# Windowed tiles of v transferred over 128 partitions instead of 112

## The chip, the cores and the metric

The kernel runs on one core of one Trainium2 chip. The metric is the device time of one execution in microseconds (us). The kernel before was timed in three runs: 497.3, 494.58 and 493.47 us, median 494.58.

## The reference, cut to what matters

Three layers follow one another. First comes an attention over q, k and v (4 batches, 8 heads, 576 positions, 64 wide) that adds a local part and a part on averaged positions:

```python
mask = np.abs(pos[:, None] - pos[None, :]) < 4
scores = np.where(mask, scale * q @ k.T, -1e9)
out_local = softmax(scores) @ v
q_d, k_d, v_d = means of 4 neighbouring positions
out_up = np.repeat(softmax(scale * q_d @ k_d.T) @ v_d, 4, axis=2)
x = out_up + out_local
```

Its output, as 2304 rows of 512, goes through `g(x @ w_in) @ w_out`, where g is a ratio of polynomials in its argument and w_in and w_out are 512x2048 and 2048x512. The result feeds a soft mixture of 8 experts (phi, w1, w2), which gives the output. Because the local part sees only 3 neighbours on each side, 32 queries need 38 positions of k and v.

## The kernel before, in words

**Attention.** The work goes in 16 pairs of heads. Each pair has three loads, all issued by SP. `load_qk` (line 538) brings q and k (`in_qk`, 128 partitions x 1158 f32). `load_v` (lines 540 to 542) brings two things: v for the averaged part (`in_vd`, 72 rows filled up to 80, x 1024 f32), which is added up over four positions on POOL (L570, L571) or DVE, and v for the local part (`in_vw`, `VROWS` = 112 rows x 1280 f32):

```python
begin(out=s.Vdl, in_=vd[bb, p])
begin(out=s.V[0:VROWS], in_=vw[bb, p])
```

`in_vw` is made on the host (lines 1531 to 1534 and 1538). v is cut into 18 overlapping tiles of 38 positions. Four tiles after four, two of them side by side, lie one above the other: the first two at partitions 0 to 37, the next two at partitions 64 to 101. The rows between and behind are zeros. TensorE reads only those two groups of 38 partitions (`av`, line 643). Line 1538 cuts the array to 112 rows.

For a pair, TensorE computes the local scores (`sc`, L576, L580) and the averaged ones (`scd`, L590). DVE takes the maxima (L595), ACT the exponentials (L598, L602), DVE and POOL the normalisation (L612, L613, L617). TensorE transposes (L623, L632) and multiplies with v (`avd` L650, `av` L643), and DVE adds both parts (L667).

**Weights.** w_in and w_out arrive as 64-bit floats, 1 MB for 256 columns or rows (`wst`, eight loads of each). DVE turns them into 32-bit floats in three steps (`nar`: L756, L761, L765). ACT and POOL split w_in further (L729, L734). w_out is stored to a tile in DRAM (`wo_dram`) and read back later.

**Order.** The order of all instructions on every engine is fixed by hand (`PLACE`), so an instruction that waits holds up all that stands behind it on its engine. SP issues nearly all transfers, in order, at line 427 (`begin`). Before some loads it also waits until an older load has landed: going back over the loads before, it adds up planned durations until they reach 4.5 us, and waits for the load found there (`LIMIT`, `GATED`, lines 353 to 359, and line 429). So a load that lands late makes a later one start late. The first four pairs use four sets of buffers and are loaded together with the first weights, in the first 55 us. From the fifth pair on each pair's loads wait until the buffers of the one before are free.

**Later.** After the first 60 us TensorE multiplies with w_in (`hps`, L889), while ACT, DVE and POOL compute g (`gate`, L965 to L994). The remaining pairs of the attention are worked in between, until about 310 us. The experts' weights (`we`, 32 loads of 1 MB) and the last layer follow.

Of the kernel before, what the change touches and what calls it, by code (L numbers as in the profile page):

```python
# [15 lines left out]
B, H, S, D = 4, 8, 576, 64  # L16
# [5 lines left out]
PAD = 3  # L22
QT = 32
WIN = QT + 2 * PAD
VROWS = 112
NEG = -8.0e9
EPS = 1e-9
COLS = ((0, 256), (256, 128), (384, 128))
# [377 lines left out]
def attn_moe_moe_kernel(ctx, tc, qk, vw, vd, w_in, w_out, w1, w2, cf, cb, out):  # L406
# [18 lines left out]
    def begin(out, in_):  # L425

        x = nc.sync.dma_start(out=out, in_=in_)
        if plan.gate.get(plan.item) in begun and plan.item not in begun:
            tc.add_manual_dep(x.ins, begun[plan.gate[plan.item]].ins.name, GATE, reason="few loads at once")
        begun[plan.item] = x  # L430
# [109 lines left out]
    def load_v(s, bb, p):  # L540
        begin(out=s.Vdl, in_=vd[bb, p])
        begin(out=s.V[0:VROWS], in_=vw[bb, p])

# [1038 lines left out]
```

## Time and profile before

| | |
|---|---|
| median of three runs | 494.58 us (493.47 to 497.3) |
| the profiled execution, its own time | 496.0 us |
| its span, from the first instruction to the last | 494.2 us |
| granted TensorE clock, mean | 0.979 |
| TensorE matmul busy | 460.3 us, 93% |
| DVE / ACT / POOL busy | 401.0 / 321.2 / 246.8 us |
| bytes moved by DMA | 88.50 MB |

Times in the trace count from the start of the span. The profiled execution took 1.8 us more than its span, and 1.4 us more than the median of the three runs. A busy share is a mean over the whole span; the first 60 us look different from the rest.

### The profile page before, as it was taken

The numbers are of one execution on the slowest core, as the hardware profiler recorded it, in microseconds if no ns is written. First come the engines' busy times: TensorE is split into PE (matmuls) and PEld (weight loads), VectorE is DVE, ScalarE is ACT, GpSimd is POOL, SyncE is SP. The second block draws the span as 40 slices with busy tenths as digits, with TensorE's granted clock in tenths as the row PEclk, the third lists the DMA queues.
The fourth block names the chain that finished last, engine by engine and source line by source line (L and its number), as shares of the span: only waits on it lengthen the run. The fifth ranks groups of instructions, "written<-read, shape, count | busy, mean of one in ns | idle before, by whom it ended". The sixth has DMA issues, their size and how long they took to land.

```text
span 494.2 us, 12949 instructions
## 1 busy us (share of the span) xinstructions
PE 460.3 (93%) x5417; PEld 335.1 (68%) x5417; DVE 401.0 (81%) x568; ACT 321.2 (65%) x682; POOL 246.8 (50%) x231
## 2 busy tenths in 40 slices
PE   7677889999999999999999999999999999799994
PEld 5455656787777777866777676777776976343574
DVE  5697999999999899958888799899899988736133
ACT  3664388788776778867779776667866576710122
POOL 6587777875874557577174656624142605101000
PEclk9799899999999999999999999999999999999898
DMA  8999915476555101312402322380000499999956
GB/s 333 299 281 319 324 51 221 138 235 215 147 156 164 52 27 53 118 51 76 122 1 76 97 61 72 128 316 1 0 1 0 165 383 354 388 426 426 426 221 237
DMA packets 17610, 88.50 MB, mean 179 GB/s; under 512 B 2064, under 2 KB 2576, under 8 KB 10896
## 3 DMA queue, kind: packets, MB, share of 16 engines
q1 hardware_dynamic: 17552, 87.67, 50.6%
q8 instruction: 43, 0.70, 0.6%
q14 instruction: 15, 0.12, 0.1%
HBM read 78.75 MB, written 8.91 MB: 177 GB/s over the span
## 4 chain that ended last, share of the span: by engine, by line
PE 42%; DVE 21%; POOL 12%; ACT 11%; DMA 9%; issue 4%; SPq 0%; DVEq 0%; POOLq 0%; ACTq 0%
PE hps L889 15%; POOL gate L971 7%; DMA at<-in_qk 5%; PE op L1451 3%; DVE gate L990 3%; ACT hps L989 3%; PE gt L1018 3%; PE hps L907 2%; DMA wst<-in_w_in 2%; POOL gate L967 2%; ACT gate L988 2%; DMA wo_dram<-wo 2%; ACT gate L975 2%; PE hp L1330 2%; PE scd L590 2%
## 5 line engine op out<-in xcount | busy, mean ns | idle before, releaser
L889 PE MATMUL hps<-XH,W 128*128 128x512 f32 x512 | 169.4, 400 | 2.4 <-DVE wst L765 1.8
L889 PEld LDWEIGHTS hps<-XH,W 128*128 128x128 f32 x512 | 96.6, 189 | 28.8 <-issue 2.5
L971 POOL TENSOR_TENSOR gate<-gate 128x1024 f32<-128x1024 f32 (+1 forms) x34 | 81.1, 2386 | 47.1 <-ACT gate L965 21.9
L889 PE MATMUL hps<-XL,W 128*128 128x512 f32 x256 | 100.7, 393 | 0.2
L967 POOL TENSOR_SCALAR gate<-gate,cf_sb 128x1024 f32<-128x1024 f32 (+1 forms) x25 | 32.2, 1289 | 71.9 <-ACT gate L975 70.4
L988 ACT ACTIVATE gate<-gate,one 128x1024 f32<-128x1024 f32 (+1 forms) x37 | 42.0, 1136 | 33.1 <-POOL gate L971 32.1
L990 DVE SCALAR_TENSOR_TENSOR gate<-gate,hps 128x1024 f32<-128x1024 f32 (+1 forms) x37 | 44.0, 1188 | 14.0 <-ACT hps L989 13.5
L889 PEld LDWEIGHTS hps<-XL,W 128*128 128x128 f32 x256 | 48.4, 189 | 9.8 <-POOL XL L734 0.9
L989 ACT ACTIVATE hps<-gate 128x1024 f32<-128x1024 f32 (+1 forms) x37 | 37.2, 1006 | 8.9 <-DVE gate L987 4.1
L729 ACT COPY G<-gt 128x512 f32<-128x512 f32 x56 | 32.7, 590 | 9.7 <-PE gt L1018 9.4
L564 POOL TENSOR_TENSOR at<-at 128x144 f32<-128x144 f32 x56 | 35.5, 634 | 4.4
L975 ACT ACTIVATE gate<-hps 128x1024 f32<-128x1024 f32 (+1 forms) x29 | 29.0, 999 | 5.4 <-PE hps L889 4.2
L971 DVE TENSOR_TENSOR gate<-gate,hps 128x1024 f32<-128x1024 f32 x24 | 29.1, 1214 | 4.0 <-ACT gate L965 3.8
L1018 PE MATMUL gt<-cf_sb,gate 128*128 128x128 f32 x192 | 28.7, 278 | 2.5 <-ACT G L729 1.1
L1018 PEld LDWEIGHTS gt<-cf_sb,gate 128*128 128x128 f32 x192 | 21.7, 141 | 11.3 <-ACT G L729 3.8
L602 ACT ACTIVATE at<-sc,at 128x38 f32<-128x38 f32 x144 | 28.2, 315 | 0.6
L987 DVE SCALAR_TENSOR_TENSOR gate<-gate,cf_sb,hps 128x1024 f32<-128x1024 f32 x22 | 28.1, 1276 | 0.6
L994 DVE SCALAR_TENSOR_TENSOR gate<-gate 128x1024 f32<-128x1024 f32 x20 | 26.0, 1298 | 0.4
L617 POOL TENSOR_TENSOR at<-at 128x432 f32<-128x432 f32 (+1 forms) x24 | 20.3, 852 | 12.0 <-DVE at L613 8.7
L965 ACT ACTIVATE gate<-hps,cf_sb 128x1024 f32<-128x1024 f32 x19 | 23.0, 1208 | 4.0 <-PE gt L1018 2.6
L907 PE MATMUL hps<-xs,W 128*128 128x256 f32 x192 | 24.3, 285 | 1.3 <-DVE A L993 1.2
L993 DVE SCALAR_TENSOR_TENSOR gate<-gate,cf_sb,hps 128x1024 f32<-128x1024 f32 x20 | 25.5, 1273 | 0.0
(182 smaller groups left out, 983.5 us busy)
## 6 DMA issues: line engine op xcount, KB each, us to landing
we<-in_w SPq DMA_DIRECT2D x32, 1024.0 KB, 9.5
at<-in_qk SPq DMA_DIRECT2D x16, 579.0 KB, 5.2
at<-in_vw SPq DMA_DIRECT2D x16, 560.0 KB, 5.2
wst<-in_w_in SPq DMA_DIRECT2D x8, 1024.0 KB, 9.5
wst<-in_w_out SPq DMA_DIRECT2D x8, 1024.0 KB, 5.9
at<-in_vd SPq DMA_DIRECT2D x16, 320.0 KB, 5.7
out<-late SPq DMA_DIRECT2D x17, 256.0 KB, 2.4
wo_dram<-wo SPq DMA_DIRECT2D x8, 512.0 KB, 8.0
```

The costliest lines, as they stand in the source:

```text
L564: nc.gpsimd.tensor_tensor(out=dst, in0=dst, in1=x[:, :, j], op=ALU.add)
L602: nc.scalar.activation(out=dst[:, i, :], in_=st["s", j][:, i, :], func=ACTF.Exp, scale=scale, bias=mx[:, i:i + 1], accum_out=None if sums ...
L729: nc.scalar.copy(out=out, in_=x)
L889: nc.tensor.matmul(hps[m][:, c].rearrange("p u t -> p (u t)"), lhsT=W[p][:, w, kk, 128 * c:128 * c + 128], rhs=x[xx][:, kk, :], start=(kk ...
L907: nc.tensor.matmul(out[:, c, :], lhsT=W[p][:, w, kk, 128 * c:128 * c + 128], rhs=xs[i][:, xx, kk, :], start=(kk == 0 and j == 0), stop=(kk ...
L967: (nc.vector if who == "d" else nc.gpsimd).tensor_scalar(out=out, in0=x, scalar1=coef[:, w:w + 1], scalar2=coef[:, b:b + 1], op0=ALU.mult, ...
L971: turned_over((nc.vector if who == "d" else nc.gpsimd).tensor_tensor(out=out, in0=x, in1=y, op=op), who)
L975: do("ab", "B", "H", lambda B, H: act(out=B, in_=H, func=ACTF.Abs, scale=coef[:, 4:5] if s2 else 1.0))
L988: do("ln", "C", "B", lambda C, B: act(out=C, in_=B, func=ACTF.Ln, bias=one))
L989: do("ex", "H", "C", lambda H, C: act(out=H, in_=C, func=ACTF.Exp, scale=-1.0))
L990: do("e", "B", "H", lambda B, H: stt(out=B, in0=B, scalar=1.0 + 1e-6, in1=H, op0=ALU.add, op1=ALU.mult))
L1018: nc.tensor.transpose(gt[n][:, u, 128 * c:128 * c + 128], g_of(n, c)[:, 128 * u:128 * u + 128], idn)
```

## The change

`VROWS` goes from 112 to 128, and the host no longer cuts the array. The tile in SBUF has 128 partitions already. Each of the 16 `in_vw` loads moves 128 x 1280 x 4 = 655,360 bytes instead of 573,440. The 16 rows more are zeros that nothing reads.

```diff
-VROWS = 112
+VROWS = 128
...
-        "vw": flat(win, B, H // 2, 128, 1280)[:, :, 0:VROWS].copy(),
+        "vw": flat(win, B, H // 2, 128, 1280),
```

The instructions of TensorE, DVE, ACT and POOL stand in the same order with the same waits. On SP only the shape of 16 rows differs. Here is the place on SP of the first of them; `at` is the buffer, the names in brackets are semaphores that the row waits for.

```order
 L427 DMA at<-in_qk 128x1158 [waits DMAHW4_49]
 L427 DMA at<-in_vd 80x1024
-L427 DMA at<-in_vw 112x1280 [waits DMAHW1_49]
+L427 DMA at<-in_vw 128x1280 [waits DMAHW1_49]
 L427 DMA wst<-in_w_in 128x2048 [waits DMAHW6_49]
```

Nothing moved: the load waits for what it waited for, and the same loads stand ahead of and behind it.

## Rows read from the trace of the kernel before

**Rows 1.** The page: DMA busy tenths in 40 slices of 12.4 us; the chain by engine.
```profile
DMA  8999915476555101312402322380000499999956
...
PE 42%; DVE 21%; POOL 12%; ACT 11%; DMA 9%; issue 4%; SPq 0%; DVEq 0%; POOLq 0%; ACTq 0%
```
**Rows 2.** Chain that ended last, 0 to 60 us: start us, us, what.
```profile
9.07 9.02 DMA at<-in_qk
...
26.56 9.19 DMA wo_dram<-wo
...
35.77 7.41 DMA at<-in_qk
...
43.19 10.76 DMA wst<-in_w_in
```
**Rows 3.** Timeline of DVE, 10 to 60 us; in brackets idle before, and its releaser.
```profile
19.57 0.52 DVE L595 TENSOR_REDUCE at<-sc 128x9 f32<-128x342 f32 x1 [1.08 <-PE sc L580]
...
23.54 0.61 DVE L595 TENSOR_REDUCE at<-scd 128x3 f32<-128x432 f32 x1 [2.32 <-PE scd L590]
...
38.16 1.23 DVE L756 TENSOR_SCALAR nar<-wst 128x1024 int32<-128x1024 int32 x1 [0.64 <-DMA wst<-in_w_in]
...
47.29 0.69 DVE L756 TENSOR_SCALAR nar<-wst 128x512 int32<-128x512 int32 x1 [2.00 <-DMA wst<-in_w_in]
...
54.05 0.69 DVE L756 TENSOR_SCALAR nar<-wst 128x512 int32<-128x512 int32 x1 [0.70 <-DMA wst<-in_w_in]
```
**Rows 4.** Busy time by stretch; last columns PEclk, DMA share, GB/s.
```profile
9.00:14.00 5.00, 3.29 (x182) 2.45 (x169) 4.34 (x9) 4.31 (x22) 3.34 (x7) 1.00 0.99 409
14.00:19.00 5.00, 1.65 (x92) 1.37 (x95) 4.15 (x9) 3.75 (x21) 1.63 (x2) 0.73 1.04 277
...
21.00:27.00 6.00, 5.26 (x102) 3.92 (x100) 3.61 (x6) 5.55 (x22) 3.95 (x7) 0.82 1.03 249
28.00:32.00 4.00, 3.48 (x33) 1.97 (x32) 3.97 (x9) 1.36 (x3) 3.48 (x3) 1.00 0.99 246
...
39.00:44.00 5.00, 4.62 (x99) 3.38 (x96) 4.86 (x5) 3.71 (x7) 1.93 (x4) 1.00 0.99 406
44.00:51.00 7.00, 3.96 (x87) 3.17 (x86) 4.86 (x9) 1.46 (x4) 6.69 (x8) 0.71 1.03 252
...
56.00:60.00 4.00, 3.97 (x18) 2.96 (x17) 3.83 (x9) 1.64 (x2) 3.44 (x4) 1.00 1.05 229
```
**Rows 5.** Timeline of SP, 0 to 60 us: the issue of transfers.
```profile
9.93 0.42 SPq L427 DMA_DIRECT2D at<-in_vw  x1
...
18.53 0.90 SPq L427 DMA_DIRECT2D at<-in_vw  x1
...
25.54 0.43 SPq L427 DMA_DIRECT2D at<-in_vw  x1
...
32.45 2.10 SPq L427 DMA_DIRECT2D wst<-in_w_in  x2
...
36.20 0.53 SPq L427 DMA_DIRECT2D wst<-in_w_in  x1
...
38.53 0.47 SPq L427 DMA_DIRECT2D at<-in_vw  x1
...
54.40 0.42 SPq L427 DMA_DIRECT2D at<-in_vw  x1
```
**Rows 6.** Tensor in_vw, 180 to 320 us (7 loads): who waited (nobody listed), and landing.
```profile
who waited for it (us, times):
busy tenths in 40 slices 0000000000000000000000000000000000000000
DMA to landing us min/median/max: 3.9/4.2/5.1
```
**Rows 7.** Tensor in_qk, 160 to 300 us (6 loads): landing.
```profile
DMA to landing us min/median/max: 3.7/3.9/5.1
```
**Rows 8.** Tensor in_vd, 160 to 320 us (7 loads): landing.
```profile
DMA to landing us min/median/max: 3.0/3.2/5.3
```

## The prediction

> **What bounds the kernel now.** I read the page's slices first, then the chain of waits, then the timelines of DVE and SP and the busy times by stretch for the first 60 us. The change touches only transfers, so the question is where transfers set the end. The DMA engines are busy at 8 to 9 tenths in the first five slices and again in the late stretch of expert weights; between them they are half idle [rows 1]. The chain has 9% of DMA, some 44 us, and most of it lies before 54 us: four of its pieces add up to 9.02 + 9.19 + 7.41 + 10.76 = 36.4 us [rows 1, 2]. After that it runs through PE, DVE, POOL and ACT.
>
> How a late transfer reaches the end is seen on DVE. In the first 60 us it has five idle gaps of note: 1.08 and 2.32 us before score maxima, and 0.64, 2.00 and 0.70 us directly for weights (`wst`) that have not landed, 6.74 us in all [rows 3]. Everything on DVE stands in a fixed order, and the weight conversions behind those gaps feed TensorE's first products. So a gap that goes moves what follows.
>
> Now the row that matters for the change. The queue is full in all of the stretches listed: the DMA share is 0.97 or more. Yet it moves 409 and 406 GB/s in two of them, and 277, 249, 246, 252 and 229 in the others [rows 4]. The slow stretches are those behind an issue of `in_vd` and `in_vw` (9.93, 18.53, 25.54, 38.53 and 54.40 us; the data follow some 2 to 6 us later, in the order of issue) [rows 5]. In the fast ones the queue carries loads and stores of 128 rows, `in_qk` and `wst`. So with the 112-row and 80-row loads in flight the same busy engines move some 0.6 of what they move otherwise, and the weights that share the queue are held back with them.
>
> Which of the two shapes is it? Later, each load lands alone or nearly so. `in_vd` (80 x 1024 x 4 = 327,680 bytes) takes 3.2 us, `in_qk` (128 x 1158 x 4 = 592,896 bytes) 3.9 us [rows 7, 8]. On the line through these two, 0.7 us for 265,216 bytes, `in_vw` with its 573,440 bytes should take 3.2 + 0.7 x 245,760 / 265,216 = 3.85 us. It takes 4.2 [rows 6], longer than the larger `in_qk`. So 112 rows are 0.35 us out of line even in a quiet queue; `in_vd` sets one end of the line, so it is not tested by it.
>
> [...]
>
> **The change part by part.** Nothing is removed from or added to any engine, and no wait changes. 16 loads grow by 81,920 bytes each.
>
> *The eleven loads after 60 us.* By the line above, 655,360 bytes over 128 rows take 3.2 + 0.7 x 327,680 / 265,216 = 4.06 us against 4.2 measured. Nobody is listed as waiting for `in_vw` [rows 6]: these cost and gain nothing.
>
> *The five early loads.* The price of a 128-row `in_vw` in a full queue is not in the trace. One end: it goes like the other 128-row loads, at about 405 GB/s. The other: the queue stays at about 250 GB/s, because the 80-row `in_vd` or the mixture causes it, and the bytes are simply added: 81,920 / 250 = 0.33 us a load. I take the first end for `in_vw` and all that shares the queue with it, and the slow rate for `in_vd` itself (328 KB / 250 = 1.31 us), since the 0.35 us above speak against the 112 rows. Then, each stretch with its bytes (rate x time), less `in_vd`, plus 82 KB, at 405 GB/s, plus 1.31 us [rows 4]:
> 14 to 19 us: 1385 KB, (1385 - 328 + 82) / 405 + 1.31 = 4.12, 0.9 us less. 21 to 27: 1494 KB, 4.39, 1.6 less. 28 to 32: 984 KB, 3.13, 0.9 less. 44 to 51: 1764 KB, 5.06, 1.9 less. Together 5.3 us of queue time before 51 us.
>
> *What of that reaches DVE.* Four terms, in order.
> 1. The fourth `in_qk` lands at 18.09 us (9.07 + 9.02) [rows 2], in the first slow stretch; TensorE's scores wait for it, and DVE for them in the gaps of 1.08 and 2.32 us [rows 3]. The stretch loses 0.9; I take 0.8, since `in_vd` still stands right behind this load. Bounds 0 and 1.9 (twice the stretch's loss, should TensorE, whose clock is at 0.73 there, also stay warm).
> 2. The gap of 0.64 us at 38.16: its weights were issued at 32.45, behind a landing that three slow stretches delay. They come over 2 us earlier, DVE only 0.8: the gap goes. 0.64, bounds 0 and 0.64.
> 3. The gap of 2.00 us at 47.29. Its load was issued at 36.20, behind the landing of `wo_dram` at 35.75 (26.56 + 9.19) [rows 2, 5]. The issue ahead of that ended at 34.55 (32.45 + 2.10) [rows 5], late because it waits for buffers that PE, ACT and POOL release, and these move only by the 0.8 of term 1. So this issue moves by 1.2 + 0.8 = 2.0. Three of the seven slow microseconds lie before its landing: 0.8 more. It comes 2.8 earlier, DVE 1.44: 1.4 of the gap goes. Bounds 0 and 2.0.
> 4. The gap of 0.70 us at 54.05. Its load was issued at 43.19 behind an `in_qk` whose issue at 35.77 moves by 2.0, and it lies in the last stretch (1.9): 3.9 earlier, DVE 2.84. It goes. 0.70, bounds 0 and 0.70.
> Sum: 0.8 + 0.64 + 1.4 + 0.7 = 3.5 us, with bounds 0 and 5.2. To the upper one belong 1.1 us more, if the fifth load, at 56 to 60 us (916 KB, 2.96 instead of 4 us), is also felt: 6.3.
>
> After 54 us the work on DVE, POOL and PE waits for one another and not for loads, so I carry the sum to the end whole. The profiled execution would take 496.0 - 3.5 = 492.5 us. It lies 1.4 above the median of the runs, so against that: 494.58 - 3.5 = 491.1 us.
>
> **The rivals.**
> *Bytes only, slower.* The 80 rows of `in_vd`, or unequal rows in one queue as such, cause the slow rate, and 128 rows bring nothing back. Its place is the full queue before 60 us; its price is 0.33 us for each of four loads before the last DVE gap, 1.3 us, straight into gaps where DVE already waits. It decides if the slow stretches stay at about 250 GB/s. For it: `in_vd` is in every slow stretch. Against it: the 0.35 us of `in_vw` in a quiet queue. Time 494.58 + 1.3 = 495.9 us. [...]
> *Hidden.* The loads become faster, but the gaps on DVE are set by other things on the way (buffers released by POOL and PE before an issue, the order on TensorE), and half a microsecond is left. For it: SP's issue that ended at 34.55 waited for buffers. Against it: three of the gaps name a landing. Time 494.1 us.
> *All of it.* With `in_vw` in line, `in_vd` hurts less as well, the early gaps go to the upper bounds and the fifth stretch counts: 494.58 - 6.3 = 488.3 us.
>
> **How the numbers follow.** My forecast gets 0.50, all of it 0.20, hidden 0.18, bytes only 0.12. A change of 1% (4.9 us) is about what a measurement of this kernel can tell. Faster by over 1% means below 489.6 us: most of "all of it" (0.17) and the lower edge of the forecast (0.08), 0.25. Slower by over 1%, above 499.5, needs more than any term here: 0.02. The rest, 0.73, is within 1%. The range runs from 487.0, a little below the largest gain, to 496.0, the bytes-only case. The forecast's own range is 489.2 to 492.8.
>
> **What would show it.** In the profile after, the stretches behind an early `in_vw` should move 330 to 400 GB/s at a full DMA share instead of 246 to 277; the first five `in_vw` should land in about 7 to 9 us; alone, a load of 128 rows in about 4.0 us, not above 4.2. The fourth `in_qk` should land near 17.2 us, and the gaps of 0.64, 2.00 and 0.70 us shrink to about 0.6 together. PE's chain after 60 us should look the same, shifted. I am wrong if the stretches stay near 250 GB/s (then bytes only), or if they reach 400 and DVE's gaps stay (then hidden).

## The result, and the profile after

The changed kernel took 492.48 us (median of 16 runs, 489.48 to 499.11), the kernel before, in 16 runs beside it and ahead of it, 497.34 us. The ratio is 0.9902, with a 95% interval of 0.9875 to 0.993: about 1.0% faster, where 0.7% was forecast (491.1 against 494.58). The same kernel timed twice more gave 0.9917 (0.988 to 0.9955) and 0.9942 (0.9907 to 0.9977). The three intervals overlap; a gain of 0.6 to 1.0%, some 3 to 5 us, covers them. The median of the three runs that the prediction started from, 494.58 us, lies 2.8 us below that of the 16, so ratios are the safer measure. Executions more than 1.5% above the fastest of their kernel count as slow and stand in no ratio, and in no median or profile of the experiments below.

The profiled execution after took 491.29 us, its span 489.4 us against 494.2. The page first: DMA slices and the chain by engine, which answer to [rows 1].

```profile
span 489.4 us, 12949 instructions
...
DMA  8999734566645102312402312380000399999966
...
PE 44%; DVE 20%; POOL 13%; ACT 11%; DMA 6%; issue 4%; SPq 0%; DVEq 0%; POOLq 0%; ACTq 0%
```

The fifth slice went from 9 to 7 tenths, and DMA fell from 9% to 6% of the chain: more bytes, less time behind them. The chain itself, 0 to 60 us (start us, us, what), against [rows 2]:

```profile
9.11 7.83 DMA at<-in_qk
...
34.04 9.99 DMA wst<-in_w_in
...
47.52 2.93 PE hps L889 x6
```

The fourth `in_qk` lands at 16.94 us instead of 18.09. The pieces of `wo_dram`, the later `in_qk` and the weights issued at 43.19 have left the chain; from 17 to 34 us and from 44 us on compute stands in it. DVE shows what that was worth; its timeline, with idle time before and its releaser in brackets, against [rows 3]:

```profile
18.41 0.52 DVE L595 TENSOR_REDUCE at<-sc 128x9 f32<-128x342 f32 x1 [0.33 <-PE sc L580]
...
22.37 0.61 DVE L595 TENSOR_REDUCE at<-scd 128x3 f32<-128x432 f32 x1 [2.31 <-PE scd L590]
...
36.60 1.23 DVE L756 TENSOR_SCALAR nar<-wst 128x1024 int32<-128x1024 int32 x1 [0.23 <-DMA wst<-in_w_in]
...
44.12 0.69 DVE L756 TENSOR_SCALAR nar<-wst 128x512 int32<-128x512 int32 x1 [0.42 <-DMA wst<-in_w_in]
...
50.10 0.68 DVE L756 TENSOR_SCALAR nar<-wst 128x512 int32<-128x512 int32 x1
...
52.73 0.23 DVE L667 TENSOR_TENSOR X<-av,at 128x64 f32<-128x64 f32 x1 [0.50 <-ACT at L654]
```

Row by row, DVE is 1.16, 1.17, 1.56, 3.17 and 3.95 us ahead of before. Then a wait for ACT, where there was none of note, takes back about 0.6, and from 53 us on it is 3.4 us ahead. ACT waited there for TensorE, which was granted a clock of 0.50 from 48 to 50 us.

The queue, by stretch (last columns PEclk, DMA share, GB/s). All stretches came earlier, so these are those of the changed kernel that lie behind an early `in_vw`, with two between them, and the whole first 60 us as the last row; compare [rows 4].

```profile
15.00:18.00 3.00, 1.71 (x100) 1.44 (x103) 2.90 (x9) 2.62 (x15) 1.63 (x2) 0.78 0.99 266
21.00:24.00 3.00, 2.11 (x21) 1.19 (x18) 1.63 (x2) 2.87 (x13) 2.60 (x4) 1.00 1.02 246
27.00:30.00 3.00, 3.00 (x12) 1.70 (x12) 3.00 (x6) 1.17 (x2) 2.42 (x2) 0.50 1.05 265
36.00:41.00 5.00, 3.75 (x30) 2.67 (x30) 4.63 (x7) 2.64 (x6) 3.91 (x6) 1.00 1.01 418
41.00:45.00 4.00, 3.64 (x90) 2.58 (x88) 3.51 (x7) 2.52 (x6) 3.82 (x4) 1.00 1.04 262
45.00:52.00 7.00, 5.84 (x141) 4.50 (x142) 6.79 (x12) 2.53 (x5) 5.83 (x7) 0.76 1.00 417
52.00:56.00 4.00, 4.00 (x47) 3.27 (x40) 3.37 (x8) 1.94 (x3) 3.62 (x4) 1.00 1.03 268
...
0.00:60.00 60.00, 49.05 (x797) 35.41 (x798) 49.48 (x92) 33.09 (x105) 44.30 (x63) 0.91 0.95 331
```

The slow stretches are still there and just as slow, 246 to 268 GB/s; they are shorter. Before they added up to 26 us (5 + 6 + 4 + 7 + 4), after to 17 us (3 + 3 + 3 + 4 + 4). These bounds are set by eye; counted in slices of 1 us from 9 to 60 us, 25 move under 320 GB/s at a full share before and 14 after. Landings of `in_vw`: in the first 60 us before, the same after, and after 180 us in the changed kernel, where [rows 6] had 4.2:

```profile
DMA to landing us min/median/max: 8.9/9.8/12.6
...
DMA to landing us min/median/max: 8.5/8.8/9.7
...
DMA to landing us min/median/max: 3.7/3.9/6.7
```

Where the 4.8 us between the two spans came from is read from the issue times of the same transfers on SP. Before:

```profile
71.64 0.35 SPq L427 DMA_DIRECT2D wst<-in_w_out  x1
...
306.57 0.31 SPq L427 DMA_DIRECT2D at<-in_vw  x1
...
474.24 4.60 SPq L427 DMA_DIRECT2D out<-late  x6
```

After:

```profile
68.28 0.33 SPq L427 DMA_DIRECT2D wst<-in_w_out  x1
...
303.98 0.33 SPq L427 DMA_DIRECT2D at<-in_vw  x1
...
470.16 9.99 SPq L427 DMA_DIRECT2D out<-late  x11
```

The lead is 3.36 us at 72 us, 2.59 at 307 and 4.08 at 474; the last 0.7 of the 4.8 us lie behind the last computation, in the last stores. 3.4 us come from the first 60 us. Some 0.8 are lost on the way, most of it near 120 us, where POOL (L562) waits 3.6 us for an `in_qk` instead of 2.9. That need not be a cost of the change: two profiles of one and the same kernel below (both loads 128 rows for the first five pairs) show this wait at 3.0 and 3.7 us. And 1.5 come at 460 us, where nothing is loaded that changed. There the kernel before shows this stretch (PEclk is the third number from the end):

```profile
458.00:464.00 6.00, 5.91 (x56) 3.99 (x60) 0.42 (x1) 0.93 (x3) 0.00 (x0) 0.72 1.01 427
```

and the kernel after, in the same 6 us, a clock of 1.00:

```profile
458.00:464.00 6.00, 5.99 (x104) 3.52 (x108) 0.00 (x0) 1.11 (x2) 0.00 (x0) 1.00 1.02 430
```

TensorE was granted 0.50 there for some 3.4 us, in the profile before and not in the profile after. Single dips of this kind stand at other places in six of the profiles below (at 303, 419, 454, 455, 459 and 463 us; the one at 419 is the change itself), and over 75 whole executions of the kernel before the mean clock runs from 0.931 to 0.984, so this step belongs to the pair of executions and not to the change. One profile against another is good to about 1.5 us here; the runs settle the rest.

### The profile page after: what moved, and what is told of

It is laid out like the page before. It is cut to its first block, busy times and chain, and to the rows that moved or that the text cites. A ratio compares the mean times of both kernels' runs of the same rounds, so it can differ in the third digit from the quotient of the medians.

```text
span 489.4 us, 12949 instructions
## 1 busy us (share of the span) xinstructions
PE 458.5 (94%) x5417; PEld 334.3 (68%) x5417; DVE 401.6 (82%) x568; ACT 321.1 (66%) x682; POOL 246.8 (50%) x231
## 4 chain that ended last, share of the span: by engine, by line
PE 44%; DVE 20%; POOL 13%; ACT 11%; DMA 6%; issue 4%; SPq 0%; DVEq 0%; POOLq 0%; ACTq 0%
PE hps L889 16%; POOL gate L971 7%; DMA at<-in_qk 4%; PE op L1451 3%; DVE gate L990 3%; PE gt L1018 3%; ACT hps L989 3%; PE hps L907 2%; POOL gate L967 2%; DMA wst<-in_w_in 2%; PE av L643 2%; ACT gate L988 2%; PE hp L1330 2%; PE tpd L632 2%; PE scd L590 2%
```

## The experiments

Each kernel was timed beside the kernel before on its chip. The table gathers them; the third column is the issue of the first load of w_out after 60 us, a mark for how far the early part has come, and the fourth TensorE's granted clock in the first 60 us. Mark and clock are from one profile of each kernel, with a dash where there is none.

| kernel | ratio to before (95%) | mark, us | clock |
|---|---|---|---|
| before | 1 | 71.64 | 0.89 |
| the change | 0.9902 (0.9875 to 0.993) | 68.28 | 0.91 |
| the change again | 0.9917 (0.988 to 0.9955) | 67.83 | 0.94 |
| the change, third | 0.9942 (0.9907 to 0.9977) | 68.29 | 0.94 |
| `in_vw` 128 for the first five | 0.9931 (0.9891 to 0.997) | 67.81 | 0.94 |
| `in_vw` 128 for the last eleven | 0.9999 (0.9965 to 1.0033) | 73.54 | 0.83 |
| `in_vw` as 112 and 16 rows | 1.0023 (0.9989 to 1.0056) | 73.79 | 0.83 |
| only `in_vd` 128 | 0.9971 (0.9934 to 1.0008) | 72.98 | 0.81 |
| both 128 | 0.9878 (0.983 to 0.9926) | 67.56 | 0.91 |
| both 128, again | 0.9866 (0.9818 to 0.9914) | - | - |
| both 128 for the first five | 0.9873 (0.9833 to 0.9913) | 65.94 | 0.94 |
| the same, again | 0.9929 (0.9894 to 0.9965) | 66.66 | 0.94 |

**The rows by themselves.** A kernel with nothing but loads, run once: 12 of one shape, then 12 of the next, and four mixtures with 1 MB loads like those of the weights (its loops, shortened).

```diff
+for rows in (128, 112, 96, 80, 64):
+    for j in range(12): load(j, rows, 1280, src[j])
+for rows, cols in ((128, 1280), (112, 1280), (128, 1024), (80, 1024)):
+    for j in range(12): load(j, 128, 2048, wide[j]) if j % 2 else load(j, rows, cols, src[j])
```

> Loads alone, none of the reference's work: nine stretches of 12 loads, up to 8 in flight. First 128, 112, 96, 80 and 64 rows of 1280 f32; then the same 128 x 2048 f32 loads as the weights in turn with 128 x 1280, with 112 x 1280, with 128 x 1024 and with 80 x 1024. Theory: 128 rows move 400 GB/s or more alone and mixed; 112, 96, 80 and 64 rows 200 to 320; the mixtures with 112 and with 80 rows 230 to 320, so that 112 rows take longer than 128 although they are fewer bytes. Rival (only bytes count): all stretches 380 GB/s or more.

Measured, a stretch inside each of the nine, in their order (the columns of the idle POOL and of PEclk come first; the last two are DMA share and GB/s):

```profile
8.00:20.00 12.00, 0.00 (x0) 1.00 1.02 419
24.00:48.00 24.00, 0.00 (x0) 1.00 1.02 270
53.00:72.00 19.00, 0.00 (x0) 1.00 1.02 260
76.00:92.00 16.00, 0.00 (x0) 1.00 1.01 255
100.00:116.00 16.00, 0.00 (x0) 1.00 1.02 208
120.00:140.00 20.00, 0.00 (x0) 1.00 1.01 419
148.00:176.00 28.00, 0.00 (x0) 1.00 1.02 314
188.00:204.00 16.00, 0.00 (x0) 1.00 1.02 422
208.00:228.00 20.00, 0.00 (x0) 1.00 1.01 330
```

The share is full in all nine, and the rate falls as soon as 112 rows stand in place of 128: from 419 to 270, then 260, 255 and 208 GB/s for 96, 80 and 64. A load of 128 rows takes 655,360 bytes / 419 = 1.56 us, one of 112 rows 573,440 / 270 = 2.12 us, one of 96 rows 491,520 / 260 = 1.89 us, one of 80 rows 409,600 / 255 = 1.61 us, one of 64 rows 327,680 / 208 = 1.58 us. So 128 rows are as cheap as 64. The mixtures show the second half: a queue of which half the loads are 128 x 2048 falls from 419 to 314 with 112-row loads between them, and from 422 to 330 (a little above what was expected) with 80-row loads. Most of this fall is the narrow load's own time. A 1 MB load at 419 GB/s, 2.50 us, and a 112-row load at 270, 2.12 us, would take 4.63 us together; at 314 GB/s the pair takes 5.17. The 0.5 us more is an estimate of what the mixture adds. Why 80 to 112 rows are slow, and why 64 rows move half of what 128 move (208 against 419 GB/s), no run shows.

**The same bytes in another shape.** Each `in_vw` is sent as two transfers that together write the same 128 rows.

```diff
-        begin(out=s.V[0:VROWS], in_=vw[bb, p])
+        begin(out=s.V[0:112], in_=vw[bb, p][0:112])
+        begin(out=s.V[112:128], in_=vw[bb, p][112:128])
```

> The same 128 rows and bytes as the change, but each in_vw sent as two transfers, of 112 rows and of the 16 rows of zeros. Theory (the shape of the one transfer counts): the queue is as slow as before behind each early load, 240 to 290 GB/s, and the time is 1.000 to 1.004 of before. Rival (what counts is that all 128 rows are written, or the bytes): as the change, 0.988 to 0.993.

Measured: 1.0023, and behind the first two early loads

```profile
13.00:18.00 5.00, 1.62 (x87) 1.07 (x77) 4.61 (x8) 4.18 (x24) 1.62 (x2) 0.78 1.03 283
20.00:26.00 6.00, 4.65 (x32) 3.29 (x30) 2.46 (x3) 3.91 (x16) 4.22 (x7) 0.78 1.03 264
```

as in [rows 4]. The whole gain is gone with the same bytes in the same places. So it is the rows of one transfer that count, and neither the bytes nor the rows written. What the second transfer, of 16 rows, costs by itself was not measured; the loads alone show the 112 rows slow without it.

**Which loads.** 128 rows for the first five pairs only (below), and for the other eleven only (the same with 128 and 112 exchanged).

```diff
-        begin(out=s.V[0:VROWS], in_=vw[bb, p])
+        rows = 128 if 4 * bb + p < 5 else 112
+        begin(out=s.V[0:rows], in_=vw[bb, p][0:rows])
```

> 128 rows for the in_vw loads of the first five pairs, 112 for the other eleven. Theory (the gain lies in the full queue before 60 us): all of it stays, 0.988 to 0.992 of before; the instructions at 60 us come 3.0 to 3.8 us earlier than in the kernel before. Rival (the eleven later loads bring a part of it): 0.994 to 0.997.

> 112 rows for the first five pairs, 128 for the other eleven. Theory: no difference, 0.998 to 1.002 of before, and the instructions at 60 us stand where they stood. Rival (the later loads bring a part): 0.994 to 0.997.

Measured: 0.9931 and 0.9999. The eleven alone bring nothing; in their profile the mark comes at 73.54 us. With the first five the mark is at 67.81 us, where the change has it (67.83 to 68.29). The 0.9931 lies between what the theory (0.988 to 0.992) and the rival (0.994 to 0.997) expected, and its interval covers both; the two marks and the 0.9999 decide. With `in_vd` left as it was, kernels whose first five `in_vw` have 112 rows reach the mark at 71.64, 73.54 and 73.79 us and those with 128 rows at 67.81 to 68.29. The profile of before that the prediction used has the earliest mark of its kind, so the change may be worth more than 3.4 us at this point; with one profile of each kernel, and a clock of 0.83 in the two late ones against 0.89, this is not shown.

**What in_vd still costs.** Its 80 rows filled up to 128 as well, alone and with the change.

```diff
-            self.Vdl = self.Vd[0:80]
+            self.Vdl = self.Vd[0:128]
...
-        return np.pad(x, [(0, 0), (0, 0), (0, 80 - x.shape[2]), (0, 0)])
+        return np.pad(x, [(0, 0), (0, 0), (0, 128 - x.shape[2]), (0, 0)])
```

> The change, and in_vd also sent over 128 rows (48 rows of zeros more, 196,608 bytes a load). Theory (rows that don't fill 128 slow the whole queue): the stretches of the first 55 us that still move about 300 GB/s after the change go to 380 to 425; the last early load of w_in lands 1 to 2 us before its 55.65 us of the changed kernel; the time is 0.988 to 0.986 of before, 0.5 to 1.5 us under the changed kernel. Rival (only bytes count): five early loads grow by 0.49 us each at 405 GB/s, the last early load lands about 2 us later, the time is 0.993 to 0.995 of before.

> Only in_vd over 128 rows, in_vw left at 112. Theory: the 112 rows of in_vw alone keep the queue at 250 to 320 GB/s behind each early load; the gain is a part of the change's, 0.993 to 0.998 of before. Rival (in_vd's 80 rows are the main cause): the stretches reach 350 or more and the time is 0.990 or less. Bytes only: 1.002 to 1.005.

With both shapes full, the queue no longer has a slow stretch:

```profile
13.00:18.00 5.00, 2.82 (x110) 2.09 (x110) 4.47 (x10) 4.07 (x23) 2.40 (x3) 0.83 1.04 427
20.00:26.00 6.00, 4.48 (x100) 3.23 (x97) 4.47 (x8) 4.94 (x20) 5.84 (x7) 1.00 1.02 419
26.00:31.00 5.00, 4.04 (x36) 2.19 (x34) 4.93 (x10) 2.36 (x5) 2.48 (x3) 1.00 1.02 388
40.00:47.00 7.00, 5.88 (x167) 4.61 (x166) 5.88 (x10) 3.86 (x8) 4.76 (x5) 0.99 1.02 429
```

The last early load of w_in lands at 49.90 us, against 55.65 with the change and 61.08 before: 5.75 us earlier, where 1 to 2 were expected. DVE waits for no weights any more in the first 60 us. Yet the mark moves only from 68.28 to 67.56, at the same clock of 0.91. With `in_vd` alone the first two stretches move 340 and 296 GB/s (250 to 320 were expected), and the time is 0.9971, with an interval that holds 1, no change:

```profile
13.00:18.00 5.00, 1.61 (x88) 1.33 (x91) 4.86 (x10) 4.61 (x26) 1.63 (x2) 0.86 1.04 340
20.00:26.00 6.00, 4.38 (x102) 3.18 (x100) 4.45 (x9) 5.53 (x22) 4.43 (x7) 1.00 1.03 296
```

So either shape is enough to slow the queue: 246 to 268 GB/s with `in_vd` left at 80 rows, 296 and 340 with `in_vw` left at 112. Filling up `in_vw` is what gave the time; what `in_vd` alone gives is not clear of noise. The bytes-only rival expected 0.993 to 0.995 with both and more than 1 with `in_vd` alone; neither came.

**A version that beats both?** The change, both shapes, and both for the first five pairs only (below, with `in_vd` filled up as above), side by side on one chip, then the first and the last of them on another.

```diff
-        begin(out=s.Vdl, in_=vd[bb, p])
-        begin(out=s.V[0:VROWS], in_=vw[bb, p])
+        n = 4 * bb + p < 5
+        begin(out=s.Vdl if n else s.Vdl[0:80], in_=vd[bb, p] if n else vd[bb, p][0:80])
+        begin(out=s.V[0:VROWS if n else 112], in_=vw[bb, p][0:VROWS if n else 112])
```

> The change itself, beside the two kernels sent with it on the same chip. 0.988 to 0.993 of before; the instructions at 60 us 3.0 to 4.2 us earlier than in the first profile of the kernel before.

> in_vw and in_vd both over 128 rows, again. Theory that transfers still hold DVE back in the changed kernel: 0.5 to 1.5 us under the changed kernel beside it. Rival (after the change compute sets the first 60 us, and what in_vd still costs is hidden): within 0.5 us of it. At 60 us the instructions stand 0.5 to 1 us ahead of the changed kernel in either case where TensorE's clock dips alike.

> Both over 128 rows for the first five pairs only, 112 and 80 rows after them. As the kernel with both everywhere, within 0.7 us, since the eleven later loads are off the path. Rival (the later loads' shape matters when in_vd has it too): 1 us or more apart.

> Both loads over 128 rows for the first five pairs, again, beside the change once more. If what in_vd still costs reaches the end: 0.8 to 1.6 us under the change. If it is hidden: within 0.5 us.

> The change once more, for the comparison with the kernel beside it: 0.988 to 0.993 of before.

Medians on the first chip: 492.19, 489.99 and 490.59 us (before 497.26); on the second 491.94 for both shapes in the first five and 492.67 for the change (before 495.64). All three comparisons lean to the kernels with both shapes, by 0.7 to 2.2 us, and their marks (65.94, 66.66, 67.56) lie ahead of the change's. But their intervals overlap the change's everywhere, so an extra gain of about 1 us is likely and not shown. All beat the kernel before. The third timing of the change, 0.9942, missed the 0.988 to 0.993 expected of it; its interval reaches into that range.

## Why the prediction was right, point by point

- **What bounds the early part.** The reading that rows of a transfer, and not bytes, set the rate of a full queue was right, and it is shown twice: by the loads alone (419 against 270 GB/s) and by the same bytes as 112 and 16 rows (no gain). Why the rows do it stays open.
- **Eleven later loads: nothing.** Right: 0.9999. Alone a load now lands in 3.9 us; 4.06 was worked out.
- **Queue time, 5.3 us by 51 us.** The weights that landed at 53.95 us (43.19 + 10.76 in [rows 2]) now land at 49.10: 4.85 us. Right in sum, wrong in its make-up. I gave the slow rate to `in_vd`'s own bytes alone, 1.31 us a load. A slow stretch still lasts 3 to 4 us, because the 80 rows slow what lies beside them (with `in_vd` at 128 rows too, the stretches move 388 to 429 GB/s), and I expected 330 to 400 GB/s there; it is 246 to 268, and over stretches as long as I reckoned them, 4.12 and 4.39 us from 14 and 20 us on, 294 and 276. So the sign that I had named for being wrong, stretches that stay near 250 GB/s, came true, and by it bytes only would have been the cause. The sign was badly chosen: it looked at the rate of a stretch, and what the change took away is the length. The five early `in_vw` landed in 8.5 to 9.7 us, at the upper edge of the 7 to 9 forecast.
- **Term 1, 0.8 us: measured 1.17.** The load landed at 16.94, a little before the 17.2 forecast. The gap of 1.08 fell to 0.33; the one of 2.32 stayed and only moved.
- **Term 2, 0.64: measured 0.39.** 0.23 of the gap stayed: the weights were issued 2.8 us earlier (29.68 against 32.45) but took 6.9 us to land instead of 5.7, so they came 1.6 us earlier and not over 2, and DVE came sooner than reckoned.
- **Term 3, 1.4: measured 1.61** (3.17 - 1.56).
- **Term 4, 0.70: measured 0.78, less 0.6 taken back** 2 us later by ACT, which waited for TensorE at a clock of 0.50. I had not looked for what is late next; but in the two other profiles of the change TensorE was granted 1.00 there, and nothing was taken back.
- **Sum 3.5, measured 3.4 in this pair of profiles.** How near each single term came is in part luck, as DVE's lead over the profile before shows in all three profiles of the change, in us, at the rows that stood at these times before:

  | | 19.57 | 23.54 | 38.16 | 47.29 | 54.05 | 56.91 |
  |---|---|---|---|---|---|---|
  | the change | 1.16 | 1.17 | 1.56 | 3.17 | 3.95 | 3.38 |
  | again | 0.95 | 1.21 | 1.93 | 3.20 | 3.96 | 3.99 |
  | third | -0.48 | -0.13 | 0.59 | 2.76 | 3.51 | 3.54 |

  In the third the fourth `in_qk` was issued at 9.48 us and landed at 18.6, no sooner than before, so term 1 gave nothing; DVE then came to the weights later, did not have to wait for them, and had made it up by 54 us. The sum, 3.4 to 4.0, is steadier than its parts, because DVE's waits for weights can swallow what came before them.
- **Carrying the sum to the end whole** was the weaker step. The lead shifted by -0.8, +1.5 and +0.7 on the way, by an `in_qk` that landed later, a clock dip in the profile before and the last stores. That the two spans differ by 4.8 us is no proof of the sum.
- **The size.** 0.7% forecast, 1.0, 0.8 and 0.6% measured; 3.5 us against some 3 to 5. That 491.1 us came within 1.4 us of 492.48 is partly luck: the base was 2.8 us low, and the gain was 4.9 us there and not 3.5. The profile used for the sum had an early mark for its kind; the other kernels with 112 rows in the first five pairs lie 1.3 to 2.2 us behind it. One part of that was only named as a bound of term 1: TensorE's clock. It was granted 0.81 to 0.89 in the first 60 us of the kernels with 112 rows in the early `in_vw` and 0.91 to 0.94 with 128, and over whole executions 0.973 on average in 75 of the kernel before and 0.982 in 35 of the change. That TensorE waits less for loads and is therefore granted 0.50 less often fits, but was only argued: no run changed the clock alone. It is not the whole gain: before and change are 3.4 us apart at the mark with clocks of 0.89 and 0.91.
- **The rivals.** Bytes only fell with the loads alone, the 112 and 16 rows and the time itself, in spite of its sign. Hidden fell with the DVE rows. "All of it" needed `in_vd` to hurt less; it did not. Where `in_vd` was filled up too, DVE waited for no weights, and the mark moved by 0.7 us, in two other profiles by 1.2 to 2.3. (The 1.1 us that it adds for the fifth load are 1.04 by its own numbers.)

## What to carry to other kernels

When a queue is busy all the time, look at its GB/s before its share: here stretches at 60% of the rate of their neighbours (246 to 268 against 417 and 418 GB/s), with a full share, were held by the shape of a transfer in them and not by bytes. For loads like these (rows of 4 to 5 KB, a full queue), try filling tiles up to all 128 partitions before saving rows of padding, and test the shape with a kernel of loads alone, which showed it in one run (419 GB/s with 128 rows, 270 with 112). And of a gain in a stretch that several engines share, expect other waits to keep some: weights that landed 5.75 us earlier moved the mark by 0.7 us, and by 2.3 at most in the other profiles with the same early loads.

## What the runs showed of the hardware that I had not expected

- A load of 112 rows cost a queue more than its own time: 1 MB loads with 112-row loads in turn move 314 GB/s where they move 419 with 128-row loads, and 5.17 us a pair is 0.5 us more than the two take at their own rates. In the kernel the slow stretches are slower still, 246 to 268 GB/s beside `in_vd` where the loads alone with 80 rows in turn move 330; why stays open.
- 64, 80 and 128 rows of 5 KB took nearly the same time, 1.58, 1.61 and 1.56 us a load in the loads alone; 96 rows took 1.89 and 112 rows most, 2.12 us.
- A single dip of TensorE's granted clock to 0.50 for some 3.4 us, at 460 us in the profile before, in the middle of a stretch where it was busy (5.91 of 6 us), moved that execution against the profile after, at 1.00 there, by about 1.5 us.
